# Routed experts' loop: both tiles' first layers, then both second layers, in each step

## The chip, the cores and the metric

The kernel runs on one core of a Trainium2 chip. Its time is the device time of that core in microseconds; the median of three runs of the kernel before is 1049.75 us (1049.19 to 1049.98). Engines are named as in the profile: TensorE is PE, VectorE is DVE, ScalarE is ACT, GpSimd is POOL, and SyncE is SP, which issues most of the transfers.

## The reference

Three stages follow each other, all in float32: a local attention, a three-branch feed-forward layer, and eight routed experts, of which each token uses one. The change lies in the third stage:

```
for e in range(E):                      # E = 8, N = 3072 tokens, D = 512, F = 1024
    mask = e_idx == e                   # the expert that each token chose
    h = np.maximum(x[mask] @ w1[e], 0.0)    # first layer, ReLU
    ye = h @ w2[e]                          # second layer
    out[mask] = gate_w[mask, None] * eom[mask, e, None] * ye
```

## The kernel before

**Rows and tiles.** While the feed-forward layer runs, each token's row (512 values, its number and its factor) is scattered to its expert's region of a buffer in memory, `xs`. The experts' work then goes in tiles of 128 rows. One expert, the one with the most tokens, has its weights in place for the whole loop (`own` = 1, weights `W[0]`, the tile `wp` in the profile). All others take turns in a second set of weights (`own` = 0, `W[1]`). A step of the loop takes one tile of each kind. Lists on the chip say which rows the next tiles start at (`rowi` for the changing expert, `owni` for the one in place) and which expert comes next; a register holds the number of steps, 13 with these inputs.

**One tile.** Every product is made three times, of high and low parts of both operands (`TERMS`), each with 512 columns. The first layer has two halves `f` of 4 x 3 products into one PSUM bank each; ACT applies the ReLU into `hm`. The result has to be transposed for the second layer (`h_T`: four PE transposes into a bank, a copy by ACT for the high part, a subtraction by DVE for the low part). The second layer has 8 x 3 products into one bank, `pd` for a tile of the changing expert and `pc` for the other. `y_out` scales the bank by each row's factor on DVE, then POOL writes the rows to their places in the output with an indirect transfer. Rows come in by `load`: SP reads the row number from the list, and issues one transfer of 257 KB into the row buffer `x2r`. `x_T` transposes them on PE (line 1354), and ACT and DVE make the two parts `xT`.

**Weights.** A step also renews the second set of weights for the next step: eight pieces of 512 KB (four of the first layer, four of the second), which lie in staging tiles by then. `split` casts each on ACT (line 1313), subtracts on DVE (line 185, `w<-ws,w`), and then has SP issue the transfer of the same piece for the step after that into the same staging tile (line 1327). A piece may be cast once the products that read the old one are issued.

**The order in a step.** `tile_body` is called twice. In the order of its lines a call does the first layer of its tile, transposes the rows of the next tile (`x_T`), loads the rows after those, then does the **last half of the second layer of the tile before** (`rest`), with the transposes of its own second half `h_T(1)` between, and then the first half of its own second layer. So each call leaves half a second layer to the next one, and behind the loop `rest` and `y_out` are run once more. The row buffer is single: each load waits for the transposes of the rows before it.

**What sets the order.** Inside a step the generators hand their instructions to `Plan`, which keeps a clock for each engine from estimated costs and always takes the instruction that could start first (weight pieces 0.3 us later than they could). What comes out is a fixed order for each engine; every engine, and SP with its transfers, then works its list strictly in that order, and waits where an operand isn't there. Two waits of this kind matter later: ACT's ReLU `hm` behind weight casts, and SP's row load behind weight pieces.

Of the kernel before, what the change touches and what calls it, by code (L numbers as in the profile page):

```python
# [14 lines left out]
AF = mybir.ActivationFunctionType  # L15
# [5 lines left out]
P = 128  # L21
# [243 lines left out]
def local_attention_moe_kernel(  # L265
# [1066 lines left out]
    T = {}  # L1332
    def fresh():
        ES_AT.written = LISTS_AT.written = 0.0
        for name in ("xr", "xT", "hr0", "hr1", "hh0", "hh1c", "hh1d", "yc", "yd", "nx", "cid", "did"):
# [10 lines left out]

    def x_T(half):

        xr = G["xr"]
        pTx = G["pTx"].rearrange("p (a b) -> p a b", b=P)  # L1350
        xh, xl = [t[:, :, half * P : (half + 1) * P] for t in G["xT"]]
        for d in range(KD):
            yield op(PE, 0.109, [T["xr"]], [T["pTx"]])
            nc.tensor.transpose(pTx[:, d, :], xr[:, d * P : (d + 1) * P], ident)
        yield op(ACT, act(D), [T["pTx"]], [T["xT"]])
        nc.scalar.copy(out=xh, in_=pTx)
        yield psum(dve(D), [T["pTx"], T["xT"]], [T["xT"]])
        sub(nc.vector, xl, pTx, xh.bitcast(F32))

    def x_ids(dst):  # L1360

        yield op(DVE, 0.16, [T["xr"]], [T["nx"]])
        nc.vector.tensor_copy(out=G[dst], in_=G["xr"][:, D:])

    def ids(src, dst):
        yield op(DVE, 0.16, [T["nx"]], [T[dst + "id"]])
        nc.vector.tensor_copy(out=G[dst + "id"], in_=G[src][:, 0:1])
        yield op(DVE, 0.16, [T["nx"]], [T[dst + "id"]])
        nc.vector.tensor_copy(out=G[dst + "co"], in_=G[src][:, 1:2])

    def h_at(n, f, tile_):
# [3 lines left out]
            return G["hh"][n][:, f - 4, s]  # L1375
        return G["hh"][n][:, 4 + f, s] if f < 2 else G["hx"][n][:, f - 2, s]

    def h_place(n, f, own):

        if f == 0:  # L1380
            return G["hh"][n][:, 0:4, :P]
        return G["hh"][n][:, 0:4, P : 2 * P] if own else G["hx"][n].rearrange("p a (b c) -> p (a b) c", b=2)

    def y_step(at, f, W, py, last):
        for m, (A_, B_) in enumerate(TERMS):
# [45 lines left out]
    GROUPS = (0, 2, 3, 1)  # L1431
    FIRST_Y = (0, 1, 4, 5, 6, 7, 2, 3)

    def rest(own, fs):

        n = "dc"[own]
        W, Wb = G["W"][1 - own], T["W"][1 - own][1]
        for f in fs:
            yield op(PE, pe(512, 3), [T[f"hh1{n}"], Wb], [T["p" + n]])
            y_step(lambda m: h_place(m, 1, own)[:, f - 4, :], f, W, G["p" + n], f == 7)  # L1440

    def tile_body(own, name, idx, pl):

        W, Wb = G["W"][1 - own], T["W"][1 - own]
        xT = [t[:, :, :P] for t in G["xT"]]
        n = "dc"[own]

        def h_T(f):
            hb = T["hh0" if f == 0 else "hh1" + n]
# [4 lines left out]
            hh, hl = [h_place(m, f, own) for m in range(2)]  # L1454
# [5 lines left out]
        for f in range(2):  # L1460
            b = slice(f * 512, (f + 1) * 512)
            ph = G["pg"][2 + f]
            for d in range(KD):
                yield op(PE, pe(512, 3), [T["xT"], Wb[0]], [T[f"pH{f}"]])
                for m, (A_, B_) in enumerate(TERMS):
                    nc.tensor.matmul(ph, lhsT=xT[A_][:, d, :], rhs=W[d][B_][:, b], start=(d + m == 0), stop=(d == KD - 1 and m == 2))  # L1466
                if f == 1:
                    pl.state("first", own, d)
                if (f, d) == (1, 1):
                    yield from h_T(0)  # L1470
            yield op(ACT, act(512), [T[f"pH{f}"]], [T[f"hr{f}"]])
            nc.scalar.activation(out=hm_t[f], in_=ph, func=AF.Relu)  # L1472
        yield from ids("nx", n)
        yield from x_ids("nx")
        yield from x_T(0)
        yield from load(name, idx)
        yield from rest(not own, (4, 5))
        yield from h_T(1)
        yield from rest(not own, (6, 7))
        pl.state("rest", not own)  # L1480
        m = "cd"[own]
        yield from y_out(m, T["p" + m], T["y" + m], T[m + "id"], True)
        for f in range(4):
            yield op(PE, pe(512, 3), [T["hh0"], Wb[1]], [T["p" + n]])
            y_step(lambda m: h_place(m, 0, own)[:, f, :], f, W, G["p" + n], False)
        pl.state("half", own)


    def pro_load():
        yield need(("es",), ("x", 2 * len(passes) - 1), *[("routed", n) for n in range(NFIRST)])  # L1490
        xbs = []
        for t in range(2):
            xb = yield take("x")
            xbs.append(xb)
            yield op(DMA, 0.6, [ES_AT])
            r = nc.sync.value_load(G["prow"][0:1, t : t + 1], min_val=0, max_val=E * REG - P)
            yield dma(P * D * 4, w=[xb])
            nc.sync.dma_start(out=xb.t, in_=xs[bass.ds(r, P), 0:D])
            yield dma(0, w=[T["nx"]])
# [6 lines left out]
        yield from ids("nx", "d")  # L1506
        yield from ids("bx", "c")
        state("px")

    def pro_1():  # L1510
# [17 lines left out]
            give("mbank", bank)  # L1528
        state("p1")
        yield need(*[("split", d) for d in range(2 * KD)])  # L1530
        bank = yield take("mbank")
        for n, f in enumerate(FIRST_Y):
            yield op(PE, pe(512, 3), [hx if f in (2, 3) else hb, T["W"][0][1]], [bank])
            y_step(lambda n: h_at(n, f, 0), f, W, bank.t, n == 7)
        plan.add(pro_out(bank), (4, 101))
        bank = yield take("mbank")
        G["pc"] = bank.t
        for f in range(4):
            yield op(PE, pe(512, 3), [hx if f in (2, 3) else hb, T["W"][0][1]], [bank])
            y_step(lambda n: h_at(n, f, 1), f, W, bank.t, False)  # L1540

    def pro_out(bank):
        yb = yield take("x")
        G["pd"], G["yd"] = bank.t, yb.t
        G["yc"] = next(t for t in x_t if t is not yb.t)
        yield from y_out("d", bank, yb, T["did"])

    def pro_next():
        yield need(("lists",), ("p1",), *[("routed", n) for n in range(NTILE)])
        xbs = []  # L1550
        for n in range(2):
            xb = yield take("x2r")
            T["xr"], G["xr"] = xb, xb.t
            yield from load(("rowi", "owni")[n], bass.ds(0, 1))
            xbs.append(xb)
        bank = yield take("bank")
        T["pTx"], G["pTx"] = bank, bank.t
        T["xr"], G["xr"] = xbs[0], xbs[0].t
        yield from x_T(0)
        yield from x_ids("nx")  # L1560
        G["xr"] = xbs[1].t


    ET = mybir.EngineType
# [130 lines left out]
```

## Time and profile before

| | |
|---|---|
| median of the runs | 1049.75 us |
| the profiled execution's own time | 1047.0 us |
| its span | 1045.5 us |
| PE busy | 954.8 us, 91% of the span |
| DVE, ACT, POOL busy | 657.2 us (63%), 491.7 us (47%), 213.9 us (20%) |
| routed loop, 13 steps | from 690 us to 1027 us |

The page's slices are 26.1 us wide, about as long as a step of the loop; the last fourteen or so are the loop. PE's products are pipelined, so a group's duration is longer than the distance to the next group's start; the distance is what a group costs, and that is what is counted below. An idle time stands in brackets with the instruction that ended it.

### The profile page before, as it was taken

The numbers are of one execution on the slowest core, as the hardware profiler recorded it, in microseconds if no ns is written. First come the engines' busy times: TensorE is split into PE (matmuls) and PEld (weight loads), VectorE is DVE, ScalarE is ACT, GpSimd is POOL, SyncE is SP. The second block draws the span as 40 slices with busy tenths as digits, with TensorE's granted clock in tenths as the row PEclk, the third lists the DMA queues.
The fourth block names the chain that finished last, engine by engine and source line by source line (L and its number), as shares of the span: only waits on it lengthen the run. The fifth ranks groups of instructions, "written<-read, shape, count | busy, mean of one in ns | idle before, by whom it ended". The sixth has DMA issues, their size and how long they took to land. (4 is left out here: it accounts for less than half of the span.)

```text
span 1045.5 us, 22007 instructions
## 1 busy us (share of the span) xinstructions
PE 954.8 (91%) x7764; PEld 845.4 (81%) x7764; DVE 657.2 (63%) x1687; ACT 491.7 (47%) x1060; POOL 213.9 (20%) x246
## 2 busy tenths in 40 slices
PE   2349989999999999999999999899999999999994
PEld 1238988898989899999999999777777777777773
DVE  5988987777876777723453336755655555555552
ACT  4456746555656566411231224335555555555551
POOL 5443422121212222200000002111111111111111
PEclk9958999999999999999999999999999999999997
DMA  8969877675876759470160103086656666666663
GB/s 270 236 123 194 228 184 178 144 152 126 168 164 137 165 123 175 104 173 22 53 250 21 41 22 101 22 269 206 199 191 202 203 204 194 198 202 197 203 203 100
DMA packets 225458, 165.92 MB, mean 159 GB/s; under 512 B 181660, under 2 KB 181660, under 8 KB 225376
## 3 DMA queue, kind: packets, MB, share of 16 engines
q1 hardware_dynamic: 221216, 152.21, 55.7%
q0 software_dynamic: 4160, 12.62, 3.3%
q8 instruction: 50, 0.82, 0.3%
q14 instruction: 32, 0.26, 0.1%
HBM read 115.90 MB, written 24.78 MB: 135 GB/s over the span
## 5 line engine op out<-in xcount | busy, mean ns | idle before, releaser
L914 PE MATMUL bank<-xT,w 128*128 128x256 f32 x2592 | 336.9, 287 | 4.7 <-DVE w L587 1.4
L914 PEld LDWEIGHTS bank<-xT,w 128*128 128x128 f32 x2592 | 318.4, 192 | 8.4 <-ACT xT L864 1.7
L185 DVE TENSOR_TENSOR w<-ws,w 128x1024 fp32r<-128x1024 f32 x99 | 122.1, 1235 | 71.0 <-issue 62.4
L1387 PE MATMUL bank<-w,hh 128*128 128x512 f32 x504 | 127.5, 403 | 11.9 <-PEq L1690 8.1
L781 ACT ACTIVATE sp<-sp,mn 128x232 f32<-128x232 f32 (+1 forms) x192 | 90.4, 472 | 68.7 <-DVE mn L774 63.4
L1387 PEld LDWEIGHTS bank<-w,hh 128*128 128x128 f32 x504 | 94.7, 192 | 31.9 <-issue 8.5
L1313 ACT CAST w<-ws 128x1024 fp32r<-128x1024 f32 x99 | 101.0, 1050 | 41.2 <-PE bank L1387 32.3
L986 PE MATMUL bank<-w,hh 128*128 128x512 f32 x432 | 110.0, 400 | 0.0
L944 DVE TENSOR_TENSOR hm<-hm,bank 128x512 f32<-128x512 f32 x72 | 49.2, 684 | 81.9 <-PE bank L914 79.7
L986 PEld LDWEIGHTS bank<-w,hh 128*128 128x128 f32 x432 | 77.7, 188 | 14.6
L1466 PE MATMUL bank<-wp,xT 128*128 128x512 f32 x312 | 78.0, 399 | 0.0
L1466 PE MATMUL bank<-w,xT 128*128 128x512 f32 x312 | 76.6, 394 | 0.3 <-DVEq L1643 0.3
L831 PE MATMUL bank<-va,aT 128*128 128x64 bf16 x1760 | 64.6, 197 | 13.1 <-DMA aT<-nat 11.7
L1472 ACT ACTIVATE hm<-bank 128x512 f32<-128x512 f32 x52 | 31.1, 598 | 91.5 <-PE bank L1466 91.5
L831 PEld LDWEIGHTS <-aT 128*128 128x128 f16 x1760 | 58.5, 101 | 17.8 <-DMA aT<-nat 13.0
L1086 POOL DMA_INDIRECT xs<-x2r,di x24 | 24.1, 1003 | 236.8 <-DVE x2s L185 154.8
L1466 PEld LDWEIGHTS bank<-wp,xT 128*128 128x128 f32 x312 | 57.6, 188 | 12.8
L1466 PEld LDWEIGHTS bank<-w,xT 128*128 128x128 f32 x312 | 57.5, 188 | 12.0 <-issue 0.7
L774 DVE CUSTOM_DVE_ANT_0 sp<-bank,bias 128x232 f32<-128x232 f32 x160 | 59.1, 389 | 6.8 <-PE bank L750 6.3
L657 POOL TENSOR_TENSOR qkn<-qkn,va 128x512 f32<-128x512 f32 x23 | 29.1, 1265 | 144.9 <-ACT va L655 132.4
L185 DVE TENSOR_TENSOR hh<-bank,hh 128x512 fp32r<-128x512 f32 x39 | 26.9, 689 | 50.4 <-ACT hh L1456 50.4
L750 PE MATMUL bank<-k,qh 64*128 64x232 f32 (+1 forms) x384 | 44.2, 320 | 9.0 <-ACT k L724 7.2
(232 smaller groups left out, 1407.5 us busy)
## 6 DMA issues: line engine op xcount, KB each, us to landing
ws<-in_moe_w_dram SPq DMA_DIRECT2D x111, 512.0 KB, 4.7
bias<-in_moe_w_dram SPq DMA_DIRECT2D x17, 512.0 KB, 4.3
x2r<-xs SPq DMA_DIRECT2D x28, 257.0 KB, 3.6
x<-xd SPq DMA_DIRECT2D x28, 256.0 KB, 3.4
xd<-xo SPq DMA_DIRECT2D x24, 256.0 KB, 2.2
qkn<-in_q_dram SPq DMA_DIRECT2D x23, 256.0 KB, 4.7
qkn<-in_k_dram SPq DMA_DIRECT2D x23, 256.0 KB, 3.9
qkn<-in_v_dram SPq DMA_DIRECT2D x23, 256.0 KB, 4.1
```

The costliest lines, as they stand in the source:

```text
L185: eng.tensor_tensor(out=out, in0=in0, in1=in1, op=ALU.subtract)
L750: nc.tensor.matmul(sc[j][:, hp, :nw_], lhsT=x, rhs=y, start=(n < 2), stop=(n >= len(terms) - 2))
L774: nc.vector.tensor_tensor_reduce(out=o[:, g:], in0=x[:, g:], in1=bias[:, pr, n0 + g :], scale=scale, scalar=low, op0=ALU.add, op1=ALU.min, ...
L781: nc.scalar.activation(out=o, in_=o, func=AF.Exp, scale=-1.0, bias=mn[:, h : h + 1], accum_out=sm[:, h : h + 1])
L831: nc.tensor.matmul(po[:, h, :], lhsT=a, rhs=V, start=(n == 0), stop=(n == len(terms) - 1))
L914: nc.tensor.matmul(pj[:, f2, :], lhsT=W[:, d, fs], rhs=X[:, d, :], start=(d + n == 0), stop=(d == KD - 1 and n == 2))
L944: nc.vector.tensor_max(out=hv, in0=hv, in1=pj)
L986: nc.tensor.matmul(bank.t, lhsT=X[:, f, t * P : (t + 1) * P], rhs=W[:, f, :], start=(f + n == 0), stop=(f == KF - 1 and n == 2))
L1313: (nc.scalar.copy if eng == ACT else nc.vector.tensor_copy)(out=h, in_=s.t)
L1387: nc.tensor.matmul(py, lhsT=at(A_), rhs=w, start=(f + m == 0), stop=(last and m == 2))
L1466: nc.tensor.matmul(ph, lhsT=xT[A_][:, d, :], rhs=W[d][B_][:, b], start=(d + m == 0), stop=(d == KD - 1 and m == 2))
L1472: nc.scalar.activation(out=hm_t[f], in_=ph, func=AF.Relu)
```

## The change

`tile_body` and `rest` give way to one `step`, which runs both tiles' first layers and then both tiles' whole second layers:

- The rows of a step's two tiles are both transposed in the step before, each right behind the first layer that used the old ones (`x_T(own)` into its own half of `xT`). The load for the second tile (`owni`) is issued behind the first tile's transposes and its rows are transposed later in the same step; the load for the first tile (`rowi`) is one place further in the list than before.
- `h_T` of a half follows nine products later (`d == 2`), in the next half; the last one stands inside the second layer.
- Both outputs leave at the end of a step. The last four weight pieces may be cast as the second layer of the first tile goes on (`second`), two products' groups at a time.
- Ahead of the loop the second tile's second layer is now finished (8 groups in place of 4) and its output written, three loads are issued in place of two, and two tiles' rows are transposed in place of one. Behind the loop nothing is left.

```diff
     def x_T(half):
 
-        xr = G["xr"]
+        xr, xb = G["xr"], T[f"xT{half}"]
         pTx = G["pTx"].rearrange("p (a b) -> p a b", b=P)
         xh, xl = [t[:, :, half * P : (half + 1) * P] for t in G["xT"]]
         for d in range(KD):
             yield op(PE, 0.109, [T["xr"]], [T["pTx"]])
             nc.tensor.transpose(pTx[:, d, :], xr[:, d * P : (d + 1) * P], ident)
-        yield op(ACT, act(D), [T["pTx"]], [T["xT"]])
+        yield op(ACT, act(D), [T["pTx"]], [xb])
         nc.scalar.copy(out=xh, in_=pTx)
-        yield psum(dve(D), [T["pTx"], T["xT"]], [T["xT"]])
+        yield psum(dve(D), [T["pTx"], xb], [xb])
         sub(nc.vector, xl, pTx, xh.bitcast(F32))
...
-    def h_place(n, f, own):
+    def h_place(n, own, f):
 
         if f == 0:
-            return G["hh"][n][:, 0:4, :P]
-        return G["hh"][n][:, 0:4, P : 2 * P] if own else G["hx"][n].rearrange("p a (b c) -> p (a b) c", b=2)
+            return G["hh"][n][:, 0:4, own * P : (own + 1) * P]
+        t = G["hh"][n][:, 4:6] if own else G["hx"][n]
+        return t.rearrange("p a (b c) -> p (a b) c", b=2)
...
-    def rest(own, fs):
...
-    def tile_body(own, name, idx, pl):
...
+    def step(nxt, then, pl):
+
+        late = []
+
+        def h_T():
+            own, f = late.pop()
+            hb = T[f"h{own}{f}"]
             pT = G["pg"][f].rearrange("p (a b) -> p a b", b=P)
             for d in range(4):
                 yield op(PE, 0.109, [T[f"hr{f}"]], [T[f"pT{f}"]])
                 nc.tensor.transpose(pT[:, d, :], hm_t[f][:, d * P : (d + 1) * P], ident)
+            hh, hl = [h_place(m, own, f) for m in range(2)]
             yield op(ACT, act(512), [T[f"pT{f}"]], [hb])
             nc.scalar.copy(out=hh, in_=pT)
             yield psum(dve(512), [T[f"pT{f}"], hb], [hb])
             sub(nc.vector, hl, pT, hh.bitcast(F32))
 
+        for own in range(2):
+            W, Wb = G["W"][1 - own], T["W"][1 - own]
+            xT = [t[:, :, own * P : (own + 1) * P] for t in G["xT"]]
+            for f in range(2):
+                b = slice(f * 512, (f + 1) * 512)
+                ph = G["pg"][2 + f]
+                for d in range(KD):
+                    yield op(PE, pe(512, 3), [T[f"xT{own}"], Wb[0]], [T[f"pH{f}"]])
+                    for m, (A_, B_) in enumerate(TERMS):
+                        nc.tensor.matmul(ph, lhsT=xT[A_][:, d, :], rhs=W[d][B_][:, b], start=(d + m == 0), stop=(d == KD - 1 and m == 2))
+                    if f == 1:
+                        pl.state("first", own, d)
+                    if d == 2 and late:
+                        yield from h_T()
+                yield op(ACT, act(512), [T[f"pH{f}"]], [T[f"hr{f}"]])
+                nc.scalar.activation(out=hm_t[f], in_=ph, func=AF.Relu)
+                late.append((own, f))
+            yield from ids("nb"[own] + "x", "dc"[own])
+            yield from x_ids("nb"[own] + "x")
+            yield from x_T(own)
+            yield from load(*(("rowi", then) if own else ("owni", nxt)))
+        for own in range(2):
+            n = "dc"[own]
+            W, Wb = G["W"][1 - own], T["W"][1 - own]
+            for f in range(8):
+                yield op(PE, pe(512, 3), [T[f"h{own}{f // 4}"], Wb[1]], [T["p" + n]])
+                y_step(lambda m: h_place(m, own, f // 4)[:, f % 4, :], f, W, G["p" + n], f == 7)
+                if f % 2:
+                    pl.state("second", own, f // 2)
+                if late and f == 1:
+                    yield from h_T()
+            yield from y_out(n, T["p" + n], T["y" + n], T[n + "id"], True)
...
-        bank = yield take("mbank")
-        for n, f in enumerate(FIRST_Y):
-            yield op(PE, pe(512, 3), [hx if f in (2, 3) else hb, T["W"][0][1]], [bank])
-            y_step(lambda n: h_at(n, f, 0), f, W, bank.t, n == 7)
-        plan.add(pro_out(bank), (4, 101))
-        bank = yield take("mbank")
-        G["pc"] = bank.t
-        for f in range(4):
-            yield op(PE, pe(512, 3), [hx if f in (2, 3) else hb, T["W"][0][1]], [bank])
-            y_step(lambda n: h_at(n, f, 1), f, W, bank.t, False)
-
-    def pro_out(bank):
+        for t in range(2):
+            bank = yield take("mbank")
+            for n, f in enumerate(FIRST_Y):
+                yield op(PE, pe(512, 3), [hx if f in (2, 3) else hb, T["W"][0][1]], [bank])
+                y_step(lambda n: h_at(n, f, t), f, W, bank.t, n == 7)
+            plan.add(pro_out("dc"[t], bank), (4, 101 + t))
+
+    def pro_out(n, bank):
         yb = yield take("x")
-        G["pd"], G["yd"] = bank.t, yb.t
-        G["yc"] = next(t for t in x_t if t is not yb.t)
-        yield from y_out("d", bank, yb, T["did"])
+        T["p" + n], T["y" + n] = bank, yb
+        G["p" + n], G["y" + n] = bank.t, yb.t
+        yield from y_out(n, bank, yb, T[n + "id"])
 
     def pro_next():
         yield need(("lists",), ("p1",), *[("routed", n) for n in range(NTILE)])
         xbs = []
-        for n in range(2):
+        for name, n in (("rowi", 0), ("owni", 0), ("rowi", 1)):
             xb = yield take("x2r")
             T["xr"], G["xr"] = xb, xb.t
-            yield from load(("rowi", "owni")[n], bass.ds(0, 1))
+            yield from load(name, bass.ds(n, 1))
             xbs.append(xb)
         bank = yield take("bank")
         T["pTx"], G["pTx"] = bank, bank.t
-        T["xr"], G["xr"] = xbs[0], xbs[0].t
-        yield from x_T(0)
-        yield from x_ids("nx")
-        G["xr"] = xbs[1].t
+        for t in range(2):
+            T["xr"], G["xr"] = xbs[t], xbs[t].t
+            yield from x_ids("nb"[t] + "x")
+            T[f"xT{t}"] = T["xT"]
+            yield from x_T(t)
+        T["xr"], G["xr"] = xbs[2], xbs[2].t
...
-        def step():
-            yield from tile_body(0, "rowi", bass.ds(nxt, 1), pl)
-            yield from tile_body(1, "owni", bass.ds(nxt, 1), pl)
-
         for s in staged:
             s.free = s.written = s.last = 0.0
             s.by = s.last_by = None
-        pl.add(step(), (0,))
+        pl.add(step(bass.ds(nxt, 1), bass.ds(then, 1), pl), (0,))
         for d in range(NPC):
-            pl.add(split(pl, 2 * NPC + d, [("first", 0, d) if d < KD else ("half", 0) if d < KD + 2 else ("rest", 0)], bass.ds(then, 1)), (2, d), HOLD_T)
+            pl.add(split(pl, 2 * NPC + d, [("first", 0, d) if d < KD else ("second", 0, d - KD)], bass.ds(then, 1)), (2, d), HOLD_T)
         with tc.manual_schedule(engines=ALL):
             pl.run()
-    with tc.manual_schedule(engines=ALL):
-        drain(rest(1, range(4, 8)))
-        drain(y_out("c", T["pc"], T["yc"], T["cid"]))
```

Where this puts things on PE, in the first half of a step. `x2r` are rows, `hm_547` is the second ReLU of the first tile, `wp` the weights in place. Before, the products between the two groups of transposes are those of the tile before:

```order
L1354 MATMUL bank_529<-ident,x2r 128x128 x4
L1387 MATMUL bank_527<-w_675,hh_1950 128x512 x2
L1387 REGISTER_ALU
L1387 MATMUL bank_527<-w_675,hh_1951 128x512
L1387 MATMUL bank_527<-w_675,hh_1950 128x512 x2
L1387 MATMUL bank_527<-w_675,hh_1951 128x512
L1453 REGISTER_ALU
L1453 MATMUL bank_526<-ident,hm_547 128x128 x4
```

Six products stand between the rows' transposes and those of `hm_547`. The same place on PE after the change:

```order
L1354 MATMUL bank_529<-ident,x2r 128x128 x4
L1461 MATMUL bank_528<-wp_6691,xT_716 128x512 x2
L1461 MATMUL bank_528<-wp_6691,xT_717 128x512
L1461 MATMUL bank_528<-wp_6691,xT_716 128x512 x2
L1461 MATMUL bank_528<-wp_6691,xT_717 128x512
L1461 MATMUL bank_528<-wp_6691,xT_716 128x512 x2
L1461 MATMUL bank_528<-wp_6691,xT_717 128x512
L1445 ISA
L1445 MATMUL bank_526<-ident,hm_547 128x128 x4
```

Now nine products of the second tile's first layer stand there. The transposes of the second rows, on PE after the change, with the last piece of the first layers ahead of them and the second layer behind:

```order
L1445 MATMUL bank_525<-ident,hm_546 128x128 x4
L1461 MATMUL bank_530<-wp_6691,xT_716 128x512 x2
L1461 MATMUL bank_530<-wp_6691,xT_717 128x512
L1354 REGISTER_ALU
L1354 MATMUL bank_529<-ident,x2r 128x128 x4
L1388 MATMUL bank_524<-w_1632,hh_1950 128x512 x2
L1388 MATMUL bank_524<-w_1632,hh_1951 128x512
```

Before, 18 products of a second layer and 24 of a first one stood between `hm_547` and these transposes; now 15 products of the first layer do. SP's list in a step, before, from the second weight piece to the fourth (`ws` are weight pieces):

```order
L1327 DMA ws_6692<-in_moe_w_dram 128x1024
L1327 ISA
L1327 DMA ws_6693<-in_moe_w_dram 128x1024
L1343 ISA
L1343 TENSOR_LOAD rowi
L1343 ISA x2
L1345 ISA
L1345 DMA x2r<-xs 128x514
L1327 ISA
L1327 DMA ws_6694<-in_moe_w_dram 128x1024
```

And after, from the second piece on:

```order
L1327 DMA ws_6692<-in_moe_w_dram 128x1024
L1327 ISA
L1327 DMA ws_6693<-in_moe_w_dram 128x1024
L1343 ISA
L1343 TENSOR_LOAD owni
L1343 ISA x2
L1345 ISA
L1345 DMA x2r<-xs 128x514
L1327 ISA
L1327 DMA ws_6694<-in_moe_w_dram 128x1024
L1343 ISA
L1343 TENSOR_LOAD rowi
```

The load that stands behind the third piece is now the one for the second tile, whose rows are transposed in the same step; the other load follows behind the fourth piece, in place of two pieces later.

## Rows read from the trace of the kernel before

**Rows 1.** Page, 40 slices: granted clock of PE, tenths of full speed.
```profile
PEclk9958999999999999999999999999999999999997
```
**Rows 2.** Waits of PE, 690 to 1045.5: us in total, times, longest us.
```profile
PE bank L1453 <- ACT hm L1472: 12.6, 13, 1.0
```
**Rows 3.** Timeline of PE, loop: start us, us, engine, line, operation, tiles, [idle before].
```profile
690.31 4.12 PE L1466 MATMUL bank<-w,xT 128*128 128x512 f32 x17 [0.28 <-DVEq L1643]
...
716.10 4.25 PE L1466 MATMUL bank<-w,xT 128*128 128x512 f32 x18
...
742.01 4.25 PE L1466 MATMUL bank<-w,xT 128*128 128x512 f32 x18
```
**Rows 4.** Timeline of all engines, 1001 to 1015, the last step's first part.
```profile
1001.14 4.25 PE L1466 MATMUL bank<-w,xT 128*128 128x512 f32 x18
...
1004.87 1.05 ACT L1313 CAST w<-ws 128x1024 fp32r<-128x1024 f32 x1
...
1005.23 0.60 PE L1453 MATMUL bank<-ident,hm 128*128 128x128 f32 x4
...
1006.50 2.94 ACT L1313 CAST w<-ws 128x1024 fp32r<-128x1024 f32 x3
1007.05 0.60 PE L1354 MATMUL bank<-ident,x2r 128*128 128x128 f32 x4
...
1007.25 3.80 SPq L1327 DMA_DIRECT2D ws<-in_moe_w_dram  x3
...
1007.40 1.62 PE L1387 MATMUL bank<-w,hh 128*128 128x512 f32 x6
...
1009.34 0.60 ACT L1472 ACTIVATE hm<-bank 128x512 f32<-128x512 f32 x1
1009.38 1.23 DVE L185 TENSOR_TENSOR w<-ws,w 128x1024 fp32r<-128x1024 f32 x1
...
1010.00 0.66 PE L1453 MATMUL bank<-ident,hm 128*128 128x128 f32 x4 [0.97 <-ACT hm L1472]
...
1012.06 0.33 SPq L1345 DMA_DIRECT2D x2r<-xs  x1
```
**Rows 5.** Timeline of all engines, 1015 to 1028, the same step's second part.
```profile
1016.20 1.53 SPq L1327 DMA_DIRECT2D ws<-in_moe_w_dram  x2
...
1020.65 0.60 PE L1354 MATMUL bank<-ident,x2r 128*128 128x128 f32 x4
...
1021.27 0.35 SPq L1345 DMA_DIRECT2D x2r<-xs  x1
```
**Rows 6.** Row loads (x2r) issued at 1012.06, 1021.27, 727.0, and 24 together.
```profile
DMA to landing us min/median/max: 4.3/4.3/4.3
...
DMA to landing us min/median/max: 2.6/2.6/2.6
...
DMA to landing us min/median/max: 4.0/4.0/4.0
...
DMA to landing us min/median/max: 2.6/3.5/4.6
```
**Rows 7.** Timeline of all engines, 1026 to 1046, behind the loop.
```profile
1026.60 1.82 POOL L1396 DMA_INDIRECT out_dram<-x,did  x1 [0.15 <-issue]
...
1035.29 4.36 PE L1387 MATMUL bank<-w,hh 128*128 128x512 f32 x12 [8.07 <-PEq L1690]
...
1041.33 1.01 POOL L1396 DMA_INDIRECT out_dram<-x,cid  x1 [0.55 <-issue]
```
**Rows 8.** PE timeline, 134 to 152; then two stretches, clock third from the right.
```profile
141.17 0.51 PE L914 MATMUL bank<-xT,w 128*128 128x256 f32 x2 [1.40 <-DVE w L587]
143.05 6.52 PE L914 MATMUL bank<-xT,w 128*128 128x256 f32 x40 [1.38 <-POOL w L185]
...
142.00:146.00 4.00, 2.95 (x17) 2.95 (x18) 3.79 (x11) 1.28 (x5) 3.20 (x3) 0.74 0.41 110
146.00:150.00 4.00, 3.57 (x25) 3.37 (x24) 2.54 (x13) 1.63 (x7) 1.21 (x1) 0.83 1.24 194
```

More of the change, by code (lines that the diff above doesn't have):

```diff
@@ L1334, in fresh @@
         ES_AT.written = LISTS_AT.written = 0.0
-        for name in ("xr", "xT", "hr0", "hr1", "hh0", "hh1c", "hh1d", "yc", "yd", "nx", "cid", "did"):
+        for name in ("xr", "xT", "xT0", "xT1", "hr0", "hr1", "h00", "h01", "h10", "h11", "yc", "yd", "nx", "bx", "cid", "did"):
             T[name] = Buf(None)
@@ L1354, in x_T @@
             nc.tensor.transpose(pTx[:, d, :], xr[:, d * P : (d + 1) * P], ident)
-        yield op(ACT, act(D), [T["pTx"]], [T["xT"]])
+        yield op(ACT, act(D), [T["pTx"]], [xb])
         nc.scalar.copy(out=xh, in_=pTx)
-        yield psum(dve(D), [T["pTx"], T["xT"]], [T["xT"]])
+        yield psum(dve(D), [T["pTx"], xb], [xb])
         sub(nc.vector, xl, pTx, xh.bitcast(F32))
     def x_ids(dst):
-        yield op(DVE, 0.16, [T["xr"]], [T["nx"]])
+        yield op(DVE, 0.16, [T["xr"]], [T[dst]])
         nc.vector.tensor_copy(out=G[dst], in_=G["xr"][:, D:])
     def ids(src, dst):
-        yield op(DVE, 0.16, [T["nx"]], [T[dst + "id"]])
+        yield op(DVE, 0.16, [T[src]], [T[dst + "id"]])
         nc.vector.tensor_copy(out=G[dst + "id"], in_=G[src][:, 0:1])
-        yield op(DVE, 0.16, [T["nx"]], [T[dst + "id"]])
+        yield op(DVE, 0.16, [T[src]], [T[dst + "id"]])
         nc.vector.tensor_copy(out=G[dst + "co"], in_=G[src][:, 1:2])
@@ L1432, in local_attention_moe_kernel @@
     FIRST_Y = (0, 1, 4, 5, 6, 7, 2, 3)
-    def rest(own, fs):
[L1436 to L1440, printed above, removed]
-    def tile_body(own, name, idx, pl):
[L1444 to L1449, printed above, removed]
+    def step(nxt, then, pl):
[3 more added lines that the diff above has]
+            hb = T[f"h{own}{f}"]
             pT = G["pg"][f].rearrange("p (a b) -> p a b", b=P)
@@ L1453, in h_T @@
                 nc.tensor.transpose(pT[:, d, :], hm_t[f][:, d * P : (d + 1) * P], ident)
-            hh, hl = [h_place(m, f, own) for m in range(2)]
+            hh, hl = [h_place(m, own, f) for m in range(2)]
             yield op(ACT, act(512), [T[f"pT{f}"]], [hb])
@@ L1458, in h_T @@
             sub(nc.vector, hl, pT, hh.bitcast(F32))
[L1460 to L1472, printed above, removed]
@@ L1473, in tile_body @@
-        yield from ids("nx", n)
-        yield from x_ids("nx")
-        yield from x_T(0)
[L1476 to L1482, printed above, removed]
-        for f in range(4):
-            yield op(PE, pe(512, 3), [T["hh0"], Wb[1]], [T["p" + n]])
-            y_step(lambda m: h_place(m, 0, own)[:, f, :], f, W, G["p" + n], False)
@@ L1486, in tile_body @@
-        pl.state("half", own)
+        for own in range(2):
[19 more added lines that the diff above has]
+            yield from load(*(("rowi", then) if own else ("owni", nxt)))
@@ L1498, in pro_load @@
             nc.sync.dma_start(out=xb.t, in_=xs[bass.ds(r, P), 0:D])
-            yield dma(0, w=[T["nx"]])
+            yield dma(0, w=[T["nb"[t] + "x"]])
             nc.sync.dma_start(out=G["nb"[t] + "x"], in_=xs[bass.ds(r, P), D:])
@@ L1505, in pro_load @@
             give("x", xb)
-        yield from ids("nx", "d")
-        yield from ids("bx", "c")
+        for t in range(2):
+            yield from ids("nb"[t] + "x", "dc"[t])
         state("px")
@@ L1530, in pro_1 @@
         yield need(*[("split", d) for d in range(2 * KD)])
-        bank = yield take("mbank")
-        for n, f in enumerate(FIRST_Y):
-            yield op(PE, pe(512, 3), [hx if f in (2, 3) else hb, T["W"][0][1]], [bank])
-            y_step(lambda n: h_at(n, f, 0), f, W, bank.t, n == 7)
-        plan.add(pro_out(bank), (4, 101))
-        bank = yield take("mbank")
-        G["pc"] = bank.t
-        for f in range(4):
-            yield op(PE, pe(512, 3), [hx if f in (2, 3) else hb, T["W"][0][1]], [bank])
-            y_step(lambda n: h_at(n, f, 1), f, W, bank.t, False)
-    def pro_out(bank):
+        for t in range(2):
[5 more added lines that the diff above has]
+    def pro_out(n, bank):
         yb = yield take("x")
-        G["pd"], G["yd"] = bank.t, yb.t
-        G["yc"] = next(t for t in x_t if t is not yb.t)
-        yield from y_out("d", bank, yb, T["did"])
+        T["p" + n], T["y" + n] = bank, yb
+        G["p" + n], G["y" + n] = bank.t, yb.t
+        yield from y_out(n, bank, yb, T[n + "id"])
     def pro_next():
@@ L1557, in pro_next @@
         T["pTx"], G["pTx"] = bank, bank.t
-        T["xr"], G["xr"] = xbs[0], xbs[0].t
-        yield from x_T(0)
-        yield from x_ids("nx")
-        G["xr"] = xbs[1].t
+        for t in range(2):
+            T["xr"], G["xr"] = xbs[t], xbs[t].t
[3 more added lines that the diff above has]
+        T["xr"], G["xr"] = xbs[2], xbs[2].t
     ET = mybir.EngineType
```

## The prediction

> **What bounds the kernel now.** The page comes first: in the slices of the routed loop, from 690 us to 1027, TensorE (PE) holds the full granted clock [rows 1], so its products have one price there. Then PE's waits in that stretch: 0.97 us in each of the 13 steps, 12.6 us together, for a ReLU on ScalarE (ACT) [rows 2]. One long wait stands behind the loop [rows 7]. The PE timeline gives the length of a step, from a step's first product to the next one's: 742.01 - 716.10 = 25.91 us [rows 3]. Then I took one step, the one that starts at 1001.14, with all engines [rows 4, 5], and count from its start.
>
> In it the first layer of tile 0 takes 18 products to 4.09, so a product of 512 columns takes 0.227. Four transposes and six products take 1.82 (4.09 to 5.91), and the transposes of the next rows 0.35 (5.91 to 6.26). So in that 1.82 the first product behind the transposes costs 0.1 more than another. At 8.86 the second transposes of tile 0 start, after the wait of 0.97: they need the second ReLU, and that stands on ACT behind three weight casts that start at 5.36 and step by 0.95, so it runs at 8.20. The wait is ACT's order, not the ReLU's own 0.60. Without the wait (and what it adds around it, some 0.2) a step would be about 24.7.
>
> On SyncE (SP) in the same step: three weight pieces are issued from 6.11 on, the third when VectorE (DVE) has finished its subtraction, which starts at 8.24 and takes 1.23; the load of the next rows (x2r) follows at 10.92 [rows 4]. It lands 4.3 later, at 15.2 [rows 6]. The second row load of the step goes out at 20.13 (1021.27), 3.5 us behind the last piece's issue [rows 5], and lands in 2.6. In another step the first kind took 4.0, and the longest of 24 loads 4.6. **The same 257 KB cost 2.6 alone and 4.0 to 4.6 behind weight pieces.** Now neither matters: rows that land at 15.2 are transposed at 19.51 (1020.65).
>
> **What the change does, part by part.**
>
> *PE's work* is the same per step: 96 products and six groups of four transposes, in another order. No gain and no loss there.
>
> *The wait for the second ReLU.* ACT's order up to that ReLU holds the same work (one ReLU, four casts, one copy of transposed rows); only the second cast and the copy change places. So the ReLU still runs at 8.0 to 8.2 and the transposes can start at 8.7 to 8.86. PE now comes later: 21 products to 4.77, transposes and 3 products to 5.90, the row transposes to 6.25, 9 products to 8.43. Left of 0.97 is 0.25 to 0.43; I take 0.35.
>
> *The row load that now sits between two transposes of one step.* Both tiles' rows are transposed inside the first layers, and there is one row buffer. So the load for tile 1 can only be issued behind tile 0's transposes (5.90), and tile 1's transposes need it landed. On SP it stands where the other load stands now, behind the third piece. DVE does the same list before that piece's subtraction (two weight subtractions, one of transposed rows, three small copies), so this ends at 9.47 as now and the load goes out at 10.92 as now. PE comes to the transposes at: 8.8, 0.4 for the ReLU's transposes, 12 products (2.9), transposes 0.35, 3 products 0.8, which is **13.2**. The load lands at 10.92 + 4.3 = 15.2; with 0.1 to be seen, PE starts at **15.3**. That is a new wait of 2.1 in every step. Bounds: 2.6, as for the load with nothing ahead (start 13.6, wait 0.4), to 4.6 (start 15.65, wait 2.4). I take 4.3, since the three pieces ahead are the same ones at nearly the same times: the first is issued when it is now, the second 0.6 earlier because its cast is, the third when it is now. The fourth piece is then issued right behind the load, at about 11.5 instead of 13.0, and can only add to the upper end.
>
> *The rest of a step*, from those transposes on: now, from 1020.65 to the loop's end at 1027.05, they are followed by 6 products, transposes and 18 products, 6.40 together [rows 5]. The new order has these and 24 products more, 5.5 by 0.227 each: 11.9. All casts of second-layer pieces lie there; they need only be done a step later, and PE's work hides them. The DVE scalings and POOL writes of both outputs end in the next step's first microseconds, before its first weight cast at 3.73 has given DVE work; PE hides them too. New step: 15.3 + 11.9 = **27.2**, so +1.3, and 13 steps give **+16.9** (bounds: 25.5, which is -5.3; 27.55, which is +21).
>
> *Ahead of the loop* PE gets 12 more products (2.73), one more group of transposes (0.45), and DVE one more output scaling of 0.75 before the loop's hand-over, on which PE's second product waits 0.28 now [rows 3]. Bounds 3.2 (the scaling hidden) to 4.0 (all of it in the way), I take **+3.5**. The third row load costs nothing: it is needed 6 us into the first step.
>
> *Behind the loop* the 12 products go away. Now the last step's products end at 1027.05 and the span at 1045.5: 18.45, of which 8.07 is PE waiting and 4.36 the products [rows 7]. New: from the last product to the output write 1.7 (1039.65 to 1041.33) to 2.1; then landing and leaving the loop. From the write at 1041.33 to the span's end it is 4.2, with no weight piece moving and no loop to leave; from the write at 1026.60 to PE's restart at 1035.29 it is 8.7, with pieces still moving. With a close-down of 1.6 behind that (4.2 less a lone landing of 2.6), the end lies 5.9 to 12.35 behind the last product; I take 9.4, about the middle, as in the new order the last piece goes out some 3 us before the last product. That is **-9.1** (-12.5 to -6.1).
>
> *The clock.* In the loop the granted clock is full, the level of 2.4 GHz [rows 1], with a wait of 0.97 in each step. Where two waits of 1.40 and 1.38 stood close together (139.8 to 143.05), the granted clock behind them was 0.74 and 0.83 in two stretches of 4 us, so 1.2 GHz for a part [rows 8]: (0.26 + 0.17) x 4 = 1.7 us lost. A wait of 2.1 lies between the two cases. Bounds: 0 to 1.7 in each step, 0 to 22 in all. I take one step in four, **+5.6**.
>
> Sum against the span of 1045.5: 16.9 + 3.5 - 9.1 + 5.6 = +16.9. That execution took 1047.0 with what lies around its span, and the median of the runs shown is 1049.75; I add the difference to the median: **1066**.
>
> **Rivals.**
> A: the row load is hidden, so the change is faster. Place: tile 1's row transposes. If the load takes 2.6, as the lone one does, the step is 25.5 and the sum -5.3 + 3.5 - 9.1 = -10.9: 1039. If it is hidden altogether, a step is 13.2 + 11.9 = 25.1, -10.5, and the sum -16.1: 1034. It decides at a landing of 3.4: there the steps cost 5.6, what the two ends of the loop give back. For it: the second piece goes out 0.6 earlier, and the old step's last two pieces no longer start a step. Against: behind the same three pieces that load took 4.0 to 4.6 [rows 6]. The Trainium skill, "DMA: Bandwidth & Descriptors", section on the anatomy of one DMA, gives a transfer a fixed cost of about 2 us plus its bytes at 436 GB/s. For 257 KB that is an estimate of 2.6; the lone load agrees to the tenth, the load behind the pieces does not, and by that rule the time would be this rival's 1039.
> B: the clock falls in every step: +11.3 + 22 = 1083. For it: the waits that did it stood at 2.8 together, not far above 2.1. Against: single waits of 1 us never did.
> C: the load lands earlier than now but not in time (3.4 to 3.8): 1048 to 1055.
> That the change doesn't do what it says I leave out: the order shows all of it.
>
> **How the numbers follow.** Forecast (load at 4.0 to 4.6, the clock down in up to half of the steps): 1055 to 1075, 0.60. A: 0.12. B: 0.20. C: 0.08, half of it within 2 us of no change. The range from 1048 to 1082 leaves out A and the top of B. 0.2% (2.1 us) is about what a measurement can tell from no change: faster 0.12, same 0.04, slower 0.84.
>
> **What would show it.** After the change the PE waits should name 13 times the row load (x2r) at line 1354, about 2 us each, and the ReLU's wait should be 0.2 to 0.4 or gone. A step should be 27 or more; x2r should go out near 10.9 and land near 15. The end behind the last product should be 6 to 12. I am wrong if PE doesn't wait for x2r, if that load lands in under 3.4, or if the granted clock in the loop stays 1.00 (then about 1061).

## The result and the profile after

The changed kernel takes **1062.19 us** (median of four runs, 1059.94 to 1064.30), against 1049.47 before, timed beside it. The ratio is **1.0128**, with a 95% interval of 1.0110 to 1.0147: slower by 12.7 us, where 16.3 were forecast and the range was 1048 to 1082. The profiled execution of the changed kernel took 1064.3 us, its span is 1062.8, 17.3 longer than that of before; the sum had said 16.9.

The granted clock over the 40 slices comes first, on the page after; it answers to [rows 1]. In the loop (from the 27th slice on) it shows 9 up to the last slice, as before; the 8 in the 26th slice, 664 to 691 us, lies ahead of the loop:

```profile
PEclk9859989999999999999999999899999999999998
```

A 9 stands for 0.90 or more, so this row can't show a fall that costs 1.6 us in a slice of 26.6, and [rows 1] alone couldn't show a full clock in the loop either. Stretches with two decimals can: before, a whole step had 1.00 (third from the right), and so had every stretch of 4 us in the loop. After the change there are falls in the loop, shown further below.

```profile
716.00:742.00 26.00, 25.03 (x122) 20.36 (x121) 15.54 (x23) 13.49 (x18) 4.94 (x5) 1.00 0.63 202
```

PE's waits from 690 us on (total, times, longest), which answer to [rows 2]. The 13 waits for the ReLU are gone from the list, 13 for the row load stand in their place, and one at the loop's entry is now for the output write ahead of it:

```profile
PE bank L1354 <- DMA x2r<-xs: 25.9, 13, 2.6
PE bank L1461 <- POOL seen L185: 1.0, 1, 1.0
```

The PE timeline of the loop, which answers to [rows 3]: the rows' transposes with their waits, and the first products of some steps. Three steps without a fall of the clock take 27.26 and 27.11 (from 725.02 on) and 27.16 (from 943.10 on):

```profile
711.50 0.63 PE L1354 MATMUL bank<-ident,x2r 128*128 128x128 f32 x4 [2.42 <-DMA x2r<-xs]
...
725.02 4.93 PE L1461 MATMUL bank<-w,xT 128*128 128x512 f32 x21
...
740.37 0.63 PE L1354 MATMUL bank<-ident,x2r 128*128 128x128 f32 x4 [2.11 <-DMA x2r<-xs]
...
752.28 4.93 PE L1461 MATMUL bank<-w,xT 128*128 128x512 f32 x21
...
779.39 4.93 PE L1461 MATMUL bank<-w,xT 128*128 128x512 f32 x21
...
795.23 0.63 PE L1354 MATMUL bank<-ident,x2r 128*128 128x128 f32 x4 [2.59 <-DMA x2r<-xs]
...
943.10 4.92 PE L1461 MATMUL bank<-w,xT 128*128 128x512 f32 x21
...
958.35 0.63 PE L1354 MATMUL bank<-ident,x2r 128*128 128x128 f32 x4 [2.02 <-DMA x2r<-xs]
...
970.26 4.93 PE L1461 MATMUL bank<-w,xT 128*128 128x512 f32 x21
```

One step with all engines, the last one, which starts at 1026.10; it answers to [rows 4]:

```profile
1026.10 4.93 PE L1461 MATMUL bank<-w,xT 128*128 128x512 f32 x21
...
1032.21 3.71 SPq L1327 DMA_DIRECT2D ws<-in_moe_w_dram  x3
...
1034.09 0.60 ACT L1467 ACTIVATE hm<-bank 128x512 f32<-128x512 f32 x1
1034.13 0.17 DVE L1363 COPY nx<-x2r 128x2 f32<-128x2 f32 x1
1034.33 1.23 DVE L185 TENSOR_TENSOR w<-ws,w 128x1024 fp32r<-128x1024 f32 x1
...
1034.74 0.66 PE L1445 MATMUL bank<-ident,hm 128*128 128x128 f32 x4
...
1037.04 0.33 SPq L1345 DMA_DIRECT2D x2r<-xs  x1
...
1041.61 0.63 PE L1354 MATMUL bank<-ident,x2r 128*128 128x128 f32 x4 [2.29 <-DMA x2r<-xs]
```

Counted from the step's start, the load goes out at 10.94 (10.92 was forecast) and PE starts on its rows at 15.51 (15.3). PE was ready at 13.22 (13.2). The chain of the work that ended last runs over this load in that step (start, us, what):

```profile
1037.04 4.43 DMA x2r<-xs
1041.47 0.14 issue
1041.61 0.63 PE bank L1354 x4
```

Behind the loop nothing is computed any more. The all-engines timeline at the end, which answers to [rows 7]: the last products end at 1053.70, the last output write goes out at 1055.36, and the span ends at 1062.8.

```profile
1048.09 5.61 PE L1388 MATMUL bank<-w,hh 128*128 128x512 f32 x24
...
1053.73 0.75 DVE L1393 TENSOR_SCALAR x<-bank,cco 128x512 f32<-128x512 f32 x1 [2.37 <-PE bank L1388]
...
1055.36 1.01 POOL L1397 DMA_INDIRECT out_dram<-x,cid  x1 [0.54 <-issue]
```

### The profile page after: what moved, and what is told of

Its sections match the earlier page's. It is cut to its first block, busy times and chain, and to the rows that moved or that the text cites. A ratio compares the mean times of both kernels' runs of the same rounds, so it can differ in the third digit from the quotient of the medians.

```text
span 1062.8 us, 22056 instructions
## 1 busy us (share of the span) xinstructions
PE 961.5 (90%) x7768; PEld 848.5 (80%) x7768; DVE 656.4 (62%) x1689; ACT 493.2 (46%) x1061; POOL 181.7 (17%) x246
## 5 line engine op out<-in xcount | busy, mean ns | idle before, releaser
L1388 PE MATMUL bank<-w,hh 128*128 128x512 f32 x504 | 130.6, 410 | 3.9 <-DVE hh L1427 3.9
L1313 ACT CAST w<-ws 128x1024 fp32r<-128x1024 f32 x99 | 101.0, 1048 | 31.6 <-PE bank L1445 10.9
L986 PE MATMUL bank<-w,hh 128*128 128x512 f32 x432 | 110.1, 400 | 0.0
L986 PEld LDWEIGHTS bank<-w,hh 128*128 128x128 f32 x432 | 77.7, 188 | 14.6
L1461 PE MATMUL bank<-wp,xT 128*128 128x512 f32 x312 | 82.3, 406 | 0.0
L185 POOL TENSOR_TENSOR seen<-x,dco 128x1 f32<-128x1 f32 x14 | 2.5, 180 | 310.2 <-DVE x L1393 295.8
L185 DVE TENSOR_TENSOR xT<-bank,xT 128x512 fp32r<-128x512 f32 x58 | 39.7, 687 | 22.8 <-ACT xT L1356 20.0
```

The source lines that it names most:

```text
L185: eng.tensor_tensor(out=out, in0=in0, in1=in1, op=ALU.subtract)
L986: nc.tensor.matmul(bank.t, lhsT=X[:, f, t * P : (t + 1) * P], rhs=W[:, f, :], start=(f + n == 0), stop=(f == KF - 1 and n == 2))
L1313: (nc.scalar.copy if eng == ACT else nc.vector.tensor_copy)(out=h, in_=s.t)
L1388: nc.tensor.matmul(py, lhsT=at(A_), rhs=w, start=(f + m == 0), stop=(last and m == 2))
```

## The experiments

The theory: of the 25.9 us that the waits show, all is due to one transfer, the load of the second tile's rows, which the change put between two transposes of the same step and which SP issues behind three weight pieces. The first rival: the weight pieces as such, or some other wait that would step into its place, hold the step at 27. The second: the old ReLU wait is what matters, and the new order has little to do with it.

### Two row buffers

Each tile gets its own buffer, so the second tile's rows are requested a step ahead.

```diff
+            T["xr"], G["xr"] = T[f"xr{own}"], G["xrs"][own]
             yield from ids("nb"[own] + "x", "dc"[own])
             yield from x_ids("nb"[own] + "x")
             yield from x_T(own)
-            yield from load(*(("rowi", then) if own else ("owni", nxt)))
+            yield from load(("rowi", "owni")[own], then)
...
-        T["xr"], G["xr"] = xbs[2], xbs[2].t
+        T["xr"], G["xr"] = xbs[0], xbs[0].t
+        yield from load("owni", bass.ds(1, 1))
+        G["xrs"] = [xbs[2].t, xbs[0].t]
```

> The changed kernel, with a row buffer for each of the two tiles: the rows of the second tile (owni) are requested right behind the transposes of the rows before them, a whole step ahead. Theory (the lost time is PE's wait for that load): the 13 waits of 1.6 to 2.6 us at line 1354, 25.9 us together, are gone, a step takes 25.0 to 25.2, the granted clock no longer falls in the loop (three falls of 1.7, 5 us), and the time is 1062.2 - 25.9 - 5 = 1031. Rival 1 (the wait only moves to the second transposes of the first tile, whose ReLU is nearly late): waits of 0.5 to 1 there, 1038 to 1044. Rival 2 (weight transfers bound the step, since DMA is busy for 0.6 to 1.0 of several stretches): a step stays near 27 with waits elsewhere, 1057 to 1062.

Measured: 1031.24 us (1028.28 to 1031.46), ratio to the kernel before 0.982 (0.980 to 0.984). Of PE's waits in the loop only the one at its entry is left, and the PE timeline gives a step of 969.94 - 944.98 = 24.96:

```profile
PE bank L1461 <- POOL seen L185: 1.0, 1, 1.0
```
```profile
944.98 4.92 PE L1461 MATMUL bank<-w,xT 128*128 128x512 f32 x21
...
969.94 4.93 PE L1461 MATMUL bank<-w,xT 128*128 128x512 f32 x21
```

The clock stayed full in every stretch of the loop. So the wait and what followed from it were worth 31 us, and no other wait of that size took its place. The profiled spans differ by 33.5 (1062.8 and 1029.3): 25.9 are the listed waits, 4.8 the three falls at 1.6, and the other 2.7 are 0.2 per step that the list leaves out. A step with a wait takes 25.16 and the wait, one without takes 24.95.

### The load one place further up in SP's list

The buffer stays single; SP is only made to issue the load ahead of the third weight piece.

```diff
-                yield need(("issued", n - 1))
+                yield need(("issued", n - 1), *([("loaded", 0)] if d == 2 else []))
...
             yield from load(*(("rowi", then) if own else ("owni", nxt)))
+            pl.state("loaded", own)
```

> The changed kernel with its single row buffer, but SP issues the second tile's row load ahead of the third weight piece in place of behind it. Theory (the place in SP's list makes the load late): it goes out about 2.2 us earlier, at 8.7 behind a step's start in place of 10.9; with two pieces ahead it lands 3.4 to 4.2 later, at 12.1 to 12.9, before PE comes for it at 13.2. The waits are gone, a step takes 25.1 to 25.3, the time is 1031 to 1034. Rival (the load lands when the pieces around it are through, wherever it stands): it still lands at 15, the wait stays at 1.5 to 2, 1055 to 1062.

Measured: 1031.65 us (1031.49 to 1032.06), the same as with two buffers. In the step that starts at 970.61 the load goes out at 979.24, so at 8.63, and lands 3.8 later at 12.4; PE comes at 983.67 (13.06) and doesn't wait (timeline of all engines, then the load's landing):

```profile
970.61 4.93 PE L1461 MATMUL bank<-w,xT 128*128 128x512 f32 x21
...
976.72 1.48 SPq L1327 DMA_DIRECT2D ws<-in_moe_w_dram  x2
...
979.24 0.33 SPq L1345 DMA_DIRECT2D x2r<-xs  x1
980.10 2.25 SPq L1327 DMA_DIRECT2D ws<-in_moe_w_dram  x2
...
983.67 0.60 PE L1354 MATMUL bank<-ident,x2r 128*128 128x128 f32 x4
...
DMA to landing us min/median/max: 3.8/3.8/3.8
```

Each byte moves as before. One place in the list of one queue is enough to turn the change from slower to faster.

### Thin weight pieces ahead of the load

```diff
-            nc.sync.dma_start(out=view(s.t), in_=src)
+            if d < 3:
+                nc.sync.dma_start(out=view(s.t)[:, :16], in_=src[:, :16])
+            else:
+                nc.sync.dma_start(out=view(s.t), in_=src)
```

> The changed kernel, in which the first three weight pieces of each step move 16 columns in place of 1024, so that these experts' weights are not renewed; all instructions, waits and issue times stay. It measures what the traffic of the three pieces costs the row load behind them. Theory (the 1.4 to 2 us over the 2.6 of a lone load come from the pieces' bytes): the load still goes out at 10.9, lands 2.6 to 2.8 later, PE waits 0.4 to 0.7 per step, the time is 1062 - 13 x 1.5 - 5 = 1037 to 1040. Rival (the place in the queue costs, not the bytes, or the buffer's own landing varies): landing stays at 3.8 to 4.6, waits 1.6 to 2.3, 1058 to 1062.

Measured: 1039.62 us (1037.99 to 1040.54), which is the 1039 that the prediction's rival A gave for a landing of 2.6. The 26 row loads of the loop now land 2.6 to 2.8 after their issue, and PE waits about half a microsecond per step ahead of the second tile's transposes (waits of PE, the second line being the first step's; then the landings of all 26):

```profile
PE bank L1357 <- DMA x2r<-xs: 6.1, 12, 0.6
PE bank L1357 <- DVE cid L1370: 0.7, 1, 0.7
...
DMA to landing us min/median/max: 2.6/2.7/2.8
```

In the changed kernel itself the 13 loads behind the pieces took 3.7 to 4.8, median 4.1, and the 13 others 2.6 to 2.8. So the 1.4 over the lone load come from the data of the three pieces ahead, and not from the load itself or its place in the list. A whole fourth piece still goes out 0.7 behind the load in this run, and adds nothing to it. The Trainium skill, "DMA: Bandwidth & Descriptors", section on the anatomy of one DMA, gives 2 us plus bytes at 436 GB/s, fitted there for transfers that GpSimd issues; for 257 KB that is an estimate of 2.6. All 26 loads of this run, which SP issues, agree with it. The formula has no term for neighbours ahead, and with three full pieces there the load took half as much again (4.1).

### The kernel before with its ReLU first

ACT's third and fourth weight cast of a step are held until the second ReLU of the first tile stands in ACT's list.

```diff
             nc.scalar.activation(out=hm_t[f], in_=ph, func=AF.Relu)
+            pl.state("relu", own, f)
...
-            pl.add(split(pl, 2 * NPC + d, [("first", 0, d) if d < KD else ("half", 0) if d < KD + 2 else ("rest", 0)], bass.ds(then, 1)), (2, d), HOLD_T)
+            pl.add(split(pl, 2 * NPC + d, [("first", 0, d)] + [("relu", 0, 1)] * (d > 1) if d < KD else [ ("half", 0) if d < KD + 2 else ("rest", 0)], bass.ds(then, 1)), (2, d), HOLD_T)
```

> The kernel before, with ACT's third and fourth weight cast of a step held until the second ReLU of the first tile is in ACT's list. Theory (that ReLU was late only by ACT's order): the 13 waits of 0.97 are gone, with some 0.2 around each; the time is 1049.5 - 12.6 - 2 = 1035 to 1037, with none of the change. Rival (the casts that are put off make a later product wait, or the rows' load that now stands ahead of the third piece delays the pieces): 1043 to 1050.

Measured: 1033.68 us (1032.80 to 1035.22), 14.9 faster than the kernel before timed beside it (1048.60). That is below the 1035 to 1037 expected, which counted from 1049.5; the saving is close to the 14.6 expected. The ReLU now runs 6.31 after the step's start (8.20 before), the wait is gone, and a step is 988.81 - 964.04 = 24.77 (timeline of all engines, and of PE):

```profile
964.04 4.25 PE L1466 MATMUL bank<-w,xT 128*128 128x512 f32 x18
...
970.35 0.60 ACT L1472 ACTIVATE hm<-bank 128x512 f32<-128x512 f32 x1
...
971.79 0.60 PE L1453 MATMUL bank<-ident,hm 128*128 128x128 f32 x4
...
988.81 4.25 PE L1466 MATMUL bank<-w,xT 128*128 128x512 f32 x18
```

13 x (25.91 - 24.77) = 14.8. What the kernel before lost in its loop is this wait, and the new order isn't needed to be rid of it.

### The load one place further down

```diff
+            yield need(*([] if own else [("issued", 2 * NPC + 3)]))
             yield from load(*(("rowi", then) if own else ("owni", nxt)))
```

> The changed kernel with the second tile's row load one place further down in SP's list, behind the fourth weight piece. It makes PE's wait longer and asks what that does to the granted clock. The load goes out at 12.3 to 12.9 in place of 10.9 and has four pieces ahead of it, landing 4.4 to 5 later: PE waits 3.6 to 4.6 per step in place of 2.0. Theory (the clock falls more often the longer the wait; 0.97 gave no fall, 2.0 gave 3 in 13): it falls in nearly every step, at 1.75 each. 1062.2 + 13 x 2.1 + 10 x 1.75 = 1107, from 1098 to 1116. Rival (falls come as often as before, they have to do with something else than the wait): 1083 to 1092.

Measured: 1092.61 us (1090.59 to 1094.18). My expectation was 14 too high, and the number stands at the rival's end; the parts tell why. The waits came out shorter than expected, 3.37 in the mean and not 4.1, because the load, issued later, landed in 3.1 to 3.8 and not in 4.4 to 5. The clock did fall more often: in 9 of 13 steps. PE's waits, then the granted clock (third column from the right) in a step with a fall and in the next one, which has none:

```profile
PE bank L1354 <- DMA x2r<-xs: 43.8, 13, 3.6
...
770.00:774.00 4.00, 2.42 (x10) 0.81 0.24 83
774.00:778.00 4.00, 4.00 (x17) 0.77 0.06 23
802.00:806.00 4.00, 4.00 (x22) 1.00 0.25 66
```

With these two, 1062.2 + 13 x (3.37 - 1.99) + 6 x 1.6 = 1090. So the rival is out as well: the falls don't come as often as before. Two sizes of mine failed: the landing, which made the waits 9.5 too long in all, and the falls, which came in 9 steps and not in all 13, about 7.

### Both repairs together

Two row buffers, and the casts held as in the repaired kernel before.

> The changed kernel with two row buffers, and ACT's third and fourth cast held until the second ReLU of the first tile is in ACT's list. With two row buffers alone a step took 24.95, the kernel before with the ReLU first took 24.77 with the same products. Theory (the 0.18 is what is left of the old wait, too short to be listed among PE's waits): a step takes 24.77, and the time is 1031.2 - 13 x 0.18 = 1028.9. Against the kernel before with the ReLU first (1033.7) this leaves the two ends of the loop, 4.8 us. Rival (the 0.18 belongs to the new order, such as one more group of transposes close to another): 1031.

Measured: **1027.79 us** (1026.24 to 1029.90), ratio 0.980 (0.978 to 0.982), the lowest median of this study. A step is 993.58 - 968.88 = 24.70 (24.77 was expected), where two buffers alone gave 24.96 (PE timeline):

```profile
968.88 4.92 PE L1461 MATMUL bank<-w,xT 128*128 128x512 f32 x21
...
993.58 4.93 PE L1461 MATMUL bank<-w,xT 128*128 128x512 f32 x21
```

So 0.26 per step was left of the old wait in the new order, unlisted among the waits.

Then the casts held, with one row buffer and the load ahead of the third piece:

> The same with one row buffer and the load ahead of the third piece. Theory: as with two buffers, 1029 to 1029.5. The third piece is now later too, as its cast is held; nothing needs it before the next step. Rival: PE comes to the second tile's rows 0.2 to 0.3 earlier and finds them not landed in some steps, 1030 to 1033.

Measured: 1027.93 us (1026.44 to 1029.55), the same, and about 1 below what I expected. In three of the 13 steps the load landed just behind PE's coming, as the rival had it, but that cost 0.3 at most. In the changed kernel, holding the two casts alone gives this version's lists instruction for instruction: the third piece's subtraction then comes later, and the planner sets the load ahead of that piece by itself. One condition on two casts would have been enough.

### Thin pieces at the end

As the version with both repairs, but the last four pieces of a step move 8 of 512 columns.

```diff
+            if d > 3:
+                nc.sync.dma_start(out=view(s.t)[:, :, :8], in_=src[:, :, :8])
```

> The version with two row buffers and the ReLU first, in which the last four weight pieces of each step move 8 of 512 columns, so that these experts' weights are not renewed; all instructions and waits stay. It asks whether the weight pieces still moving behind the last product belong to the 9.3 us from there to the end of the span, as the working of the prediction had left open. Theory (they don't: the last output write, landed, and the engines' leaving set the end): the end stays 9.0 to 9.5 behind the last product and the time within 1 us of 1027.8. Rival (the write shares the way with the last pieces and lands late): the end comes 1.5 to 3 earlier, 1025 to 1026.

Measured: 1028.00 us (1026.18 to 1029.64), no difference. The last products start at 1009.16, take 5.61, and the span ends at 1023.9: 9.1 behind them, as in the changed kernel (1053.70 to 1062.8, 9.1). The end is 7.4 behind the issue of the last write in both:

```profile
1009.16 5.61 PE L1391 MATMUL bank<-w,hh 128*128 128x512 f32 x24
...
1016.44 1.01 POOL L1400 DMA_INDIRECT out_dram<-x,cid  x1 [0.54 <-issue]
```

The last four pieces' bytes have no part in it.

## Why the prediction was right

| step of the working | forecast | measured |
|---|---|---|
| issue of the second tile's load, from the step's start | 10.92 | 10.94 |
| its landing | 4.3 (2.6 to 4.6) | 4.1 (3.7 to 4.8) |
| PE ready for the rows | 13.2 | 13.22 |
| new wait per step | 2.1 (0.4 to 2.4) | 1.99 (1.55 to 2.59) |
| what is left of the ReLU wait | 0.35 (0.25 to 0.43) | 0.26 |
| a step without a fall of the clock | 27.2 | 27.1 (mean of ten) |
| falls of the clock | 1 step in 4, 1.72 each | 3 of 13, 1.6 each |
| end of the span behind the last product | 9.4 (5.9 to 12.35) | 9.1 |
| ahead of the loop | +3.5 (3.2 to 4.0) | +5.7, of which 3.5 are work and 0.7 waiting |
| span | +16.9 | +17.3 |
| time | 1066 | 1062.19 |

**The mechanism** is shown from four sides. With the load a step earlier or one place further up the wait is gone; with less ahead of it the wait shrinks by 1.5 as the landing does; one place further down it grows by 1.4, for an issue 2.0 later and a landing 0.6 shorter. The bound above, 4.6, was too narrow by 0.2 for the longest landing.

**The clock.** With waits of 2.0 it fell three times, to a mean of 0.74 to 0.83 in two neighbouring stretches of 4 us each (windows of PE; the clock is third from the right, the pair from 738 is a step without a fall):

```profile
710.00:714.00 4.00, 2.50 (x10) 0.78 0.44 136
714.00:718.00 4.00, 4.00 (x18) 0.79 0.06 24
738.00:742.00 4.00, 1.89 (x12) 1.00 0.57 184
742.00:746.00 4.00, 4.00 (x21) 1.00 0.25 65
```

1 step in 4 was a choice between two bounds, and that it came out so near is luck as much as working. The number of falls per 13 steps over all runs: none at waits of 0.5 and 0.97, three at 2.0, nine at 3.4. Rival B, a fall in every step, was wrong at 2.0. The Trainium skill, "TensorE: Matmul & The Clock Gate", section on the oscillation of the clock, describes a loop in which a wait for a DMA brings the clock down in every turn; here waits of 2.0 did so in 3 of 13 turns and waits of 3.4 in 9. Which ones isn't decided by the length of the single wait: 2.59 at 795.23 gave no fall, 1.99 at 875.97 did. That stays open.

**The loop's entry** is the one term outside its bounds. PE work ahead of the loop grew by 14.56 - 10.41 = 4.15 in the traces, but 0.7 of this is the first 18 products. They stand behind a wait of 3.9 in both kernels, and ran longer at a lower granted clock in this execution: 6.51 at 0.52 and 0.63 in the two stretches of 4 us from 678, against 5.81 at 0.73 and 0.85 before. The kernel before with its ReLU first took 6.50 there, too. The 3.45 left are the forecast. What was missed is the wait behind it: PE's second product in the loop waits 0.97, now for POOL's part in the added output write, where it waited 0.28 for DVE [rows 3]. I had costed the DVE scaling there, and not the POOL instruction behind it (the timeline before the loop, then in it):

```profile
680.04 6.68 PE L1388 MATMUL bank<-w,hh 128*128 128x512 f32 x18 [3.86 <-DVE hh L1427]
...
694.60 0.40 PE L1461 MATMUL bank<-w,xT 128*128 128x512 f32 x1
695.96 4.82 PE L1461 MATMUL bank<-w,xT 128*128 128x512 f32 x20 [0.97 <-POOL seen L185]
```

**The two ends together** were to give back 5.6. The versions with the repaired loops put a number to it: 1033.68 in the old order, 1027.79 in the new one, of which 13 x 0.07 are the steps, so 5.0. That the end came out near 9.4 is luck in part. The working took a close-down of 1.6 behind the last write's landing, and the middle of two bounds for the rest because pieces would still be moving. The write goes out 1.7 behind the last product, it lands 2.8 after its issue, in the kernel before too, and 4.7 more pass behind the landing; thin pieces change none of it.

**Where the 3.8 between forecast and median went.** By the sum it is 4.5: 1049.75 + 16.9 is 1066.65, and the 1066 of the prediction is 0.65 below its own terms. The terms fit the span within 0.4, but their errors cancel. The loop's entry and what lies ahead of it added 5.7 (3.5 forecast): 3.45 of work, 0.7 of waiting, 0.7 for the clock of the 18 products, and 0.8 ahead of these (680.04, against 679.22), which no run explains. The steps without the falls added 16.2 (16.9), the falls 4.8 (5.6), and the end gave back 9.3 (9.1). Besides, the profiled execution of before lay 2.7 below the median that I added the sum to (1047.0 and 1049.75), and the profiled one of after lies 2.1 above its own (1064.3 and 1062.19). The four executions of the changed kernel have spans of 1062.8, 1058.2, 1062.7 and 1058.5 us with mean clocks of 0.970, 0.973, 0.969 and 0.975. Two or three falls of the clock fewer in the shorter ones would make up the difference of 4.4; only one execution has a trace, so this is an argument and not shown.

## What to carry to other kernels

When a buffer's next load moves closer to its use, write down three times for the new place: when the queue comes to it, when it lands behind what is in flight there, and when the consumer is ready. Take the landing from the same neighbours, and not from the lone transfer: 4.1 against 2.6 decided the sign here, as the thin pieces show. Before a loop is written in another order to be rid of a wait, move the one instruction that is late: a condition on two casts gave 15 us of the 21 that were found, and the new order gave the other 6 only with the load put right.

## What the runs showed that I had not expected

One place in SP's list is worth 31 us in one direction (1062.2 to 1031.7) and 30 in the other (1092.6). The load is also not slowest where most pieces stand ahead of it: behind two pieces it took 3.2 to 4.0, behind three 3.7 to 4.8, behind four, but 2.0 us later, 3.1 to 3.8; which of the pieces were still moving by then I did not follow. And from the last output write to the end of the span it is 7.4 with the loop's exit between, 4.2 without it [rows 7]. The write lands after 2.8 in both, so the 3 us lie behind the landing; I put them down to leaving the loop, and no run shows that by itself.
